# Outer products of a convolution kernel's tables on 64x32 array tiles, fewer of them issued alone, and wider vector operations

## The chip, the cores and the metric

The kernel runs on one core of one Trainium2 chip. The metric is the device time of one execution in microseconds. Before the change the median of three runs is 1099.31 us (1099.19 to 1099.48).

## The reference, cut to what matters

```python
def _A_ref(u, log_A_real, A_imag, C_real, C_imag, log_dt, D_skip):     # u: [1, 2048, 576], tables: [576, 128]
    dt = jnp.exp(log_dt)
    A = -jnp.exp(log_A_real) + 1j * A_imag
    C = (C_real + 1j * C_imag) * dt[:, None]
    P = jnp.exp((A * dt[:, None])[:, :, None] * pos[None, None, :])
    K = 2.0 * jnp.einsum("dn,dnl->dl", C, P).real                      # one filter of 2048 taps per channel
    y = irfft(rfft(u_t, 2 * L) * rfft(K, 2 * L))[:, :, :L]             # causal convolution, channel by channel
    return y + u * D_skip

def reference(...):
    xn = layernorm(A_u)
    s = _A_ref(xn, ...)
    g = silu(gelu(layernorm(xn) @ w1 + b1) @ w2 + b2)                  # 576 -> 4608 -> 576
    return x + s * g
```

Two bodies of work meet only in the last line: a gated two-layer network (by far the most multiplications), and a long convolution whose filter K is itself computed, for every channel, from 128 complex modes.

## The kernel before, in words

**The network.** The tokens are taken in four blocks of 512 (`TB`), two at a time, the hidden units in 12 groups of 3 x 128 (`NG`, `G`). One of the 48 slots is one group for one block: `layer1` (L617) makes three 128x512 results in PSUM, `hidden` (L653, L656, L659) turns each into gelu and splits it into a high and a low float32r part, and `layer2` (L680) multiplies these by the second weights; VectorE adds the result to `acc` (L690). Every product is made of three float32r products, high x high, high x low and low x high.

**The convolution** goes through a transform of 32 x 64 points in chunks of `CH` = 96 channels, six in all (`chunk`). Per chunk: `x1` (L1099) and `k1` (L1130) are the first stage, on the input and on the filter; `s2` (L1160) is the second, on array tiles of 64 rows and 32 columns, followed by the complex products in frequency (`copy`, `prod`, `sums`, L1169 to L1182); `inverse` (L1202) goes back, on tiles of 32 rows and 64 columns; `i1` (L1228) is the last stage. Between stages data is turned by 32x32 transposes (L1107, L1138, L1213).

**The filter's tables.** Channels are taken in 36 blocks of 16 (`SB`). `load_par` (L896, GpSimd's DMA queue) fetches the block's parameters, the 128 modes on the 128 partitions. `tables` then makes phases (L914 to L926), sines (L931, L933), magnitudes (L939) and, in `weigh` (L950 to L956), two weighted tables: `U` (32 columns per channel) and `v` (64 columns per channel), each with a real and an imaginary part. `kgen` (L995) makes each channel's filter as an outer product over the modes, U by v: 2048 taps as 32 x 64. It is 32 float32 matmuls per block, each contracting over all 128 partitions into 32 columns of the array, so four channels stand side by side. ScalarE copies the result out (L1000). `w` has two buffers; `U` and `v` have one each, so the weighing of block b waits for the product of block b-1.

**The order of the work** is fixed when the program is built. `Order` keeps a model time of each engine with durations written by hand, and pins every engine's instructions into the order in which it places them. The layer matmuls form the backbone. After them `pe_turns` looks at the steps of the other lines that TensorE must do. A step of `x1`, `k1`, `s2` or `i1` may carry a guest: `ride` takes the next ready product of `kgen`, and `lead` issues it into the spare columns (384 to 511) of the host's own PSUM tile. A product that finds no host is issued alone after `ALONE` = 12 us of model time past the moment it was ready, or after 3 us if the next block's sines have been placed and the block is due (`DUE`). `KG` = 1.03 us is what the model adds to a host for a guest.

Line numbers are those of the profile. The functions that the diff touches:

Of the kernel before, what the change touches and what calls it, by code (L numbers as in the profile page):

```python
# [18 lines left out]
P = 128  # L19
# [3 lines left out]
CH = 96  # L23
# [187 lines left out]
def mixer_kernel(ctx, tc, u, log_a_real, a_imag, c_real, c_imag, log_dt, d_skip, w1, b1, w2, b2,  # L211
# [38 lines left out]
    idp = sb.tile([P, P], F32, name="idp")  # L250
# [112 lines left out]

    def table_memory():

        t = [sb.tile([P, 2, SB, NV], F32, name="w", bufs=2) for _ in range(2)]
        t = [x.rearrange("p k c t -> p (k c t)") for x in t + [sb.tile([P, 2, SB, 64], F32, name="v")]]
        return [t[k // 3][:, k % 3 * D:(k % 3 + 1) * D] for k in range(8)]
# [418 lines left out]
    def params():  # L787
# [8 lines left out]
        dt = sb.tile([P, 2, SB, 32], F32, name="U").rearrange("p a b c -> p (a b c)")[:, :D]  # L796
# [94 lines left out]
    def load_par(b):  # L891
        if b == NB:
            return
        PAR[b] = sb.tile([P, SB, NPAR], F32, name="par", bufs=2)

        nc.gpsimd.dma_start(PAR[b].rearrange("p (g i) k -> p g (i k)", g=4), dram(  # L896
            par_s, (b // 3 * 48 + b % 3 * 4) * NPAR, [[D * NPAR, P], [12 * NPAR, 4], [1, 4 * NPAR]]))
# [7 lines left out]
    def tables(b):  # L905

        T = {}

        def phase(k):
            if k == 0:
                T["w"] = sb.tile([P, 2, SB, NV], F32, name="w", bufs=2)
                nc.vector.tensor_mul(T["w"][:, 1], bc(PAR[b][:, :, 0], 2, NV), bc(tv, 1, SB))  # L914
            else:
                u = T["w"][:, 1, :, 33:]
                nc.vector.tensor_add(u, u, bc(PAR[b][:, :, 1], 2, 32))

        def whole():
            nc.scalar.activation(T["w"][:, 0].bitcast(I32), T["w"][:, 1], AF.Copy)  # L920

        def frac():
            nc.vector.tensor_sub(T["w"][:, 1], T["w"][:, 1], T["w"][:, 0].bitcast(I32))

        def fold():
            nc.scalar.activation(T["w"][:, 0], T["w"][:, 1], AF.Abs)  # L926

        def sin(k):
            w = T["w"][:, k]
            if k == 0:  # L930
                nc.scalar.activation(w, w, AF.Sin, bias=halfpi[:, 0:1], scale=-TWO_PI)  # L931
            else:
                nc.scalar.activation(w, w, AF.Sin, scale=TWO_PI)  # L933

        def mags(k):
            if k == 0:
                T["m"] = sb.tile([P, SB, NM], F32, name="mg")
            n, e1, e8 = ((8, E1, E8), (4, E64, E512))[k]
            nc.vector.tensor_mul(T["m"][:, :, 64 * k:64 * k + 8 * n].rearrange("p c (i j) -> p c i j", i=n),  # L939
                                 bc(PAR[b][:, :, e8:e8 + n], 3, 8), bc(PAR[b][:, :, e1:e1 + 8], 2, n))  # L940

        def weigh(k, part):

            if k == 0 and part == 0:
                T["v"] = sb.tile([P, 2, SB, 64], F32, name="v")
                T["U"] = sb.tile([P, 2, SB, 32], F32, name="U")
                TAB[b] = (T["U"], T["v"])
            w, v, m = T["w"], T["v"], T["m"]
            if part == 0:
                nc.vector.tensor_mul(T["U"][:, k], w[:, k, :, 33:], m[:, :, 64:])  # L950
            elif part == 1:
                nc.vector.tensor_mul(v[:, k, :, :32], w[:, k, :, 32:0:-1], m[:, :, :32])
            elif k == 0:
                nc.vector.tensor_mul(v[:, k, :, 32:], w[:, k, :, :32], m[:, :, 32:64])
            else:
                nc.vector.scalar_tensor_tensor(v[:, k, :, 32:], w[:, k, :, :32], -1.0, m[:, :, 32:64],  # L956
                                               op0=OP.mult, op1=OP.mult)

        n = SB * 32
        f = lambda g, *a: lambda: g(*a)  # L960
        return ([step(None, 10.0 if b < 6 else 4.5, lambda: load_par(b), mark=("par", b), need=[("pack", b * SB // PK)]
                      + ([("mags", b - 2)] if b > 1 else [("xn", k) for k in range(8, NT)])),
                 step("DVE", dve(SB * NV), f(phase, 0), need=[("wu", b - 2, 1)] if b > 1 else []),
                 step("DVE", dve(n), f(phase, 1)), step("ACT", act(SB * NV), whole),
                 step("DVE", dve(SB * NV), frac), step("ACT", act(SB * NV), fold, mark=("fold", b))],
                [step("ACT", act(SB * NV), f(sin, 0), need=[("fold", b)], mark=("sin", b, 0), tbl="sin"),
                 step("ACT", act(SB * NV), f(sin, 1), mark=("sin", b, 1), tbl="sin")],
                [step("DVE", dve(2 * n), f(mags, 0), need=[("par", b)]),
                 step("DVE", dve(n), f(mags, 1), mark=("mags", b))]
                + [step("DVE", dve(n), f(weigh, k, part), need=[("sin", b, k)] + ([("kg", b - 1)] if b else []),  # L970
                        mark=("wu", b, k) if part == 2 else None) for k in range(2) for part in range(3)])

# [9 lines left out]
    def kgen(b):  # L982
# [3 lines left out]
        def mm(tile=None):  # L986
# [5 lines left out]
            for i in range(SB // 4):  # L992
                for ri in range(2):
                    for g in range(4):
                        nc.tensor.matmul(q[32 * g:32 * g + 32, i // 2, i % 2 * 64:i % 2 * 64 + 64], U[:, ri, 4 * g + i, :],  # L995
                                         v[:, ri, 4 * g + i, :], start=ri == 0, stop=ri == 1, skip_group_check=True)
# [6 lines left out]
        return [step("PE", KG + 0.2, mm, need=need + [("wu", b, 1)], cv=1, mark=("kg", b)),  # L1003
# [23 lines left out]
    def chunk(c):  # L1027
# [41 lines left out]
        def in_parts(which, i, get, m, need):  # L1069

            def high():
                a = sb.tile([P, 2, 4 * CH], F32R, name="pr").rearrange("p t c -> p (t c)")
                b = sb.tile([P, 2, 4 * CH], F32R, name="ys", bufs=2).rearrange("p t c -> p (t c)")
                PARTS2[which, i] = [t.rearrange("p (c b) -> p c b", b=m) for t in (a, b)]
                nc.scalar.activation(PARTS2[which, i][0], get(), AF.Copy)

            def low():
                a, b = PARTS2[which, i]
                nc.vector.tensor_sub(b, get(), a.bitcast(F32))

            n = 768 if which == "k" else 2000
            four.append(step("ACT", act(n), high, need=need))
            four.append(step("DVE", dve(n), low, mark=(which + "p", c, i)))

        def x1(i):
# [3 lines left out]
            def mm():  # L1089
# [4 lines left out]
                lead(q)  # L1094
                for n, (f, x) in enumerate(((0, a), (0, b), (1, a))):
                    for e in range(2):
                        for v in range(2):
                            r = slice(64 * v, 64 * v + 64)
                            nc.tensor.matmul(Q[24 * v][:, e], FP[0][r, f, 0], x[r, 12 * e:12 * e + 12],  # L1099
                                             start=n == 0, stop=n == 2, skip_group_check=True)  # L1100
            add("PE", X1, mm, cv=2, mark=("x1", c, i), need=[("xp", c, i)])
            if i + 1 < CH // 48:
                four.append(step(None, 5.0, lambda: load(i + 1), mark=("xl", c, i + 1)))
            for d0 in (0, 24):
                for e in range(2):
                    c0 = 48 * i + d0 + 12 * e
                    add("DVE", 0.65, lambda d0=d0, e=e, c0=c0: nc.vector.transpose(  # L1107
                        A2[:, :, 0, c0:c0 + 12].rearrange("p k d r -> p d k r"), Q[d0][:, e]), cv=-e)

        def k1(i):  # L1110
# [7 lines left out]
            in_parts("k", i, lambda: KT[c, i], 64, [("k1", c, i - 1) if i else ("x1", c, CH // 48 - 1)])  # L1118
# [18 lines left out]
            for g in range(4):  # L1137
                add("DVE", 0.65, lambda g=g: nc.vector.transpose(  # L1138
                    A2[:, :, 1, 48 * i + 12 * g:48 * i + 12 * g + 12].rearrange("p k d r -> p d k r"),
                    Q[g // 2 * 2][:, g % 2]),  # L1140
                    cv=-(g % 2))

        def s2(p):
# [5 lines left out]
            def mm():  # L1149
# [5 lines left out]
                for i in range(2):  # L1155
                    for ri in range(2):
                        for q in range(4):
                            for f in range(2):
                                r = slice(64 * f, 64 * f + 64)
                                nc.tensor.matmul(Q[i][32 * q:32 * q + 32, f, 2 * ri:2 * ri + 2],  # L1160
# [6 lines left out]
            def copy(i):  # L1167
                KK[i] = sb.tile([P, 2, 2, CH], F32, name="kk")
                nc.scalar.activation(KK[i], Q[i][:, :, 1::2], AF.Copy)  # L1169

            def prod(i):

                PR[i] = sb.tile([P, 2, 4 * CH], F32, name="pr").rearrange("p t (a b d) -> p t a b d", a=2, b=2)
                for t in range(2):
                    nc.vector.tensor_mul(PR[i][:, t], bc(Q[i][:, t, 0::2], 2, 2), bc(KK[i][:, t], 1, 2))

            def sums(i):
# [3 lines left out]
                nc.vector.tensor_sub(y[:, i, 0], x[:, :, 0, 0], x[:, :, 1, 1])  # L1181
                nc.vector.tensor_add(y[:, i, 1], x[:, :, 0, 1], x[:, :, 1, 0])  # L1182
            for i in range(2):
                two.append(step("ACT", act(4 * CH), lambda i=i: copy(i), need=[("s2", c, p)]))
                two.append(step("DVE", 0.95, lambda i=i: prod(i), cv=-1))
                two.append(step("DVE", 0.63, lambda i=i: sums(i), mark=("sum", c, p) if i else None))
# [548 lines left out]
```

## Time and profile before

| | |
|---|---|
| median of the runs | 1099.31 us |
| the profiled execution | 1101.59 us, its span 1099.8 us |
| TensorE matmuls | busy 99% of the span, granted clock 0.999 |
| TensorE weight loads | 87% |
| VectorE, ScalarE, GpSimd | 84%, 63%, 17% |
| DMA | 138 MB, 126 GB/s on average |
| products of `kgen` | 2304 records of 219 ns |

A matmul's busy time includes its passage through the array, so consecutive matmuls overlap: what one costs is read from start to start. Tiles of the array work side by side, and their records overlap too. A float32 matmul of the source appears as two records, a float32r matmul as one; each record of a matmul has a weight load of its own beside it, listed as PEld.

### The profile page before, as it was taken

The page shows a single profiled execution, that of the slowest core. Times are in us where ns is not written, and L with a number is a line of the kernel's source. Part 1 is how long each engine was busy: PE and PEld are TensorE (multiplying, and loading weights), DVE is VectorE, ACT ScalarE, POOL GpSimd, SP SyncE. Part 2 cuts the span into 40 slices and gives each one's busy share as a digit, 9 for nine tenths or more (in the row PEclk, how much of TensorE's full clock was granted, in tenths as well). Part 3 has the DMA queues.
Part 4 walks back from the last instruction along what each step waited for, and adds up shares of the span by engine and source line. Part 5 has one row for each costly group of instructions (what it writes and reads, how often), then busy time and mean ns, then how long its engine had stood idle before and what let it go on. Part 6 is the DMA issues. An engine that isn't in the chain of part 4 may idle for free.

```text
span 1099.8 us, 27208 instructions
## 1 busy us (share of the span) xinstructions
PE 1089.1 (99%) x11445; PEld 953.2 (87%) x11445; DVE 918.8 (84%) x1514; ACT 698.0 (63%) x1044; POOL 184.0 (17%) x255
## 2 busy tenths in 40 slices
PE   8999999999999999999999999999999999999997
PEld 7889989889888888888898888888888888888897
DVE  7698678979998899999999998898998986766356
ACT  6485699867667675676865857566775754324233
POOL 4557211161110100001100000000100012110220
PEclk9999999999999999999999999999999999999999
DMA  8836656735434252355623315242333426453453
GB/s 222 242 131 169 219 173 197 215 71 130 152 115 152 53 112 57 100 128 149 154 51 95 96 56 126 39 143 59 94 89 78 145 66 178 117 178 107 128 148 94
DMA packets 139651, 138.23 MB, mean 126 GB/s; under 512 B 88952, under 2 KB 105016, under 8 KB 138952
## 3 DMA queue, kind: packets, MB, share of 16 engines
q1 hardware_dynamic: 124664, 85.49, 29.6%
q0 software_dynamic: 14384, 50.27, 14.8%
q8 instruction: 89, 1.46, 0.6%
q10 hardware_dynamic: 480, 0.74, 0.3%
q14 instruction: 34, 0.28, 0.1%
HBM read 102.17 MB, written 36.63 MB: 126 GB/s over the span
## 4 chain that ended last, share of the span: by engine, by line
PE 95%; DMA 2%; SPq 2%; DVE 1%; issue 0%; ACTq 0%; ACT 0%; DVEq 0%
PE mxb L680 21%; PE mxa L680 21%; PE mxa L617 20%; PE mxb L617 20%; PE cv L995 3%; PE cv L1160 3%; PE cv L1202 2%; PE cv L1228 2%; PE cv L1130 1%; PE cv L1099 1%; SPq L808 1%; DMA w<-in_A_u_dram 1%; DMA acc<-in_A_u_dram 0%; DVE st L407 0%; DMA h<-in_B_b_dram 0%
## 5 line engine op out<-in xcount | busy, mean ns | idle before, releaser
L659 DVE TENSOR_TENSOR hl<-h,hh 128x512 fp32r<-128x512 f32 x144 | 98.8, 689 | 89.0 <-ACT hh L656 88.3
L680 PE MATMUL mxb<-w2h,hl 128*128 128x288 f32 x576 | 170.2, 295 | 1.8 <-DVE hl L659 1.8
L680 PE MATMUL mxb<-w2h,hh 128*128 128x288 f32 x576 | 171.6, 298 | 0.0
L680 PE MATMUL mxa<-w2h,hh 128*128 128x288 f32 x573 | 170.8, 298 | 0.0
L680 PE MATMUL mxb<-w2l,hh 128*128 128x288 f32 x576 | 169.5, 294 | 0.0
L680 PE MATMUL mxa<-w2h,hl 128*128 128x288 f32 x573 | 169.2, 295 | 0.0
L680 PE MATMUL mxa<-w2l,hh 128*128 128x288 f32 x573 | 168.6, 294 | 0.0
L653 ACT ACTIVATE h<-mxa,b1t 128x512 f32<-128x512 f32 x73 | 50.2, 689 | 110.9 <-PE mxa L617 109.9
L680 PEld LDWEIGHTS mxa<-w2h,hh 128*128 128x128 f32 x573 | 107.6, 188 | 6.6 <-issue 3.5
L680 PEld LDWEIGHTS mxb<-w2h,hh 128*128 128x128 f32 x576 | 108.1, 188 | 5.7 <-issue 1.8
L680 PEld LDWEIGHTS mxb<-w2h,hl 128*128 128x128 f32 x576 | 108.1, 188 | 2.3 <-DVE hl L659 2.3
L680 PEld LDWEIGHTS mxb<-w2l,hh 128*128 128x128 f32 x576 | 108.1, 188 | 0.6
L680 PEld LDWEIGHTS mxa<-w2l,hh 128*128 128x128 f32 x573 | 107.6, 188 | 0.7
L680 PEld LDWEIGHTS mxa<-w2h,hl 128*128 128x128 f32 x573 | 107.5, 188 | 0.1
L896 POOL DMA_DIRECT2D par<-par_s x36 | 27.8, 773 | 462.9 <-DVE mg L939 458.4
L656 ACT ACTIVATE hh<-h 128x512 fp32r<-128x512 f32 x144 | 90.6, 630 | 3.6
L653 ACT ACTIVATE h<-mxb,b1t 128x512 f32<-128x512 f32 x71 | 48.9, 689 | 68.8 <-PE mxb L617 66.4
L690 DVE TENSOR_TENSOR acc<-mxa,acc 128x576 f32<-128x576 f32 x87 | 65.5, 752 | 31.2 <-PE mxa L680 30.9
L617 PE MATMUL mxa<-XH,w1h 128*128 128x512 f32 x284 | 79.1, 400 | 0.0
L690 DVE TENSOR_TENSOR acc<-mxb,acc 128x576 f32<-128x576 f32 x88 | 66.1, 752 | 15.2 <-PE mxb L680 14.8
L617 PE MATMUL mxb<-XH,w1h 128*128 128x512 f32 x280 | 77.7, 399 | 0.0
L617 PE MATMUL mxa<-XL,w1h 128*128 128x512 f32 x284 | 76.1, 390 | 0.0
(269 smaller groups left out, 2483.8 us busy)
## 6 DMA issues: line engine op xcount, KB each, us to landing
raw<-in_B_w_dram SPq DMA_DIRECT2D x72, 288.0 KB, 3.4
raw<-in_B_w_dram SPq DMA_DIRECT2D x96, 192.0 KB, 3.8
par_s<-A POOLq DMA_DIRECT2D x4, 2160.0 KB, 8.2
par<-par_s POOLq DMA_DIRECT2D x36, 240.0 KB, 3.4
f2t<-f2q SPq DMA_DIRECT2D x24, 256.0 KB, 3.4
g2t<-g2p SPq DMA_DIRECT2D x24, 256.0 KB, 4.1
bias<-XR SPq DMA_DIRECT2D x42, 128.0 KB, 3.7
raw<-in_B_w_dram SPq DMA_DIRECT2D x48, 96.0 KB, 3.9
```

Source lines behind the costliest of these rows:

```text
L617: nc.tensor.matmul(q, a, b, start=j == 0 and i not in BEGUN, stop=j == len(ops) - 1, skip_group_check=True)
L653: nc.scalar.activation(t, q, AF.Gelu_apprx_tanh, bias=b1t[:, k:k + 1], scale=1.0)
L656: LAST[0] = nc.scalar.activation(hh[:, i], t, AF.Copy)
L659: nc.vector.tensor_sub(hl[:, i], t, hh[:, i].bitcast(F32))
L680: nc.tensor.matmul(q[:, dh, :288], a[:, i, c], b[:, i, d], start=i == 0 and k == 0 and not alone, stop=i == G - 1 and k == 2)
L690: nc.vector.tensor_add(o, q[:, dh:dh + n, :288], b)
L808: nc.sync.dma_start(r[32 * g:32 * g + 32].rearrange("c (b n) -> c b n", n=32), dram(src[k], 32 * g, [[N, 32], [32 * N, D // 32], [1, 32]]))
L896: nc.gpsimd.dma_start(PAR[b].rearrange("p (g i) k -> p g (i k)", g=4), dram(par_s, (b // 3 * 48 + b % 3 * 4) * NPAR, [[D * NPAR, P], [12 * ...
L995: nc.tensor.matmul(q[32 * g:32 * g + 32, i // 2, i % 2 * 64:i % 2 * 64 + 64], U[:, ri, 4 * g + i, :], v[:, ri, 4 * g + i, :], start=ri == ...
L1160: nc.tensor.matmul(Q[i][32 * q:32 * q + 32, f, 2 * ri:2 * ri + 2], m[r, 4 * i + q, 32 * ri:32 * ri + 32], A2[r, 4 * p + 2 * i + q // 2, :, ...
L1202: nc.tensor.matmul(QI[q // 2][64 * f:64 * f + 64, q % 2, i], MAT["g2t", p + i // 2][r, i % 2, f, ri], YS[p + i // 2][0][r, i % 2, ri, f], ...
L1228: nc.tensor.matmul(Q[h][64 * y:64 * y + 64, t], g1t.rearrange("p a e -> p (a e)"), A2[:, k:k + 2, 1].rearrange("p i d r -> p i r d"), star ...
```

## The change

- `kgen`: each outer product is split over the modes into two halves of 64, so that it runs on tiles of 64 rows by 32 columns; partitions 0 to 63 work for one half of the block's channels, 64 to 127 for the other. Four matmuls (real and imaginary, two halves) now add into one result where there were two. `load_par` places the parameters accordingly, with four DMAs per block, each with half as long runs.
- `U` and `v` disappear as tiles of their own. `w` is 32 columns wider, holds both, and still has two buffers; `weigh` works in place, in four operations rather than six. The phases of block b now wait for the product of block b-2, and the weighing no longer waits for a product.
- `ALONE` goes from 12 to 20 us, and the shorter wait now needs the next block's tables to be finished.
- `x1` issues its guest behind its own matmuls rather than ahead of them. Its input is first turned by one more ScalarE copy into `xt`; the split into parts then reads it straight.
- Pairs of VectorE operations are joined: transposes after `x1` and `k1`, the two halves of `prod`, the difference and the sum in `sums` (with a negated copy on ScalarE). `s2` writes its output in another order for this.
- Memory is laid out anew: `idp` shares the buffer of `f2t`, `dt` that of `ys`, and the rows held in table memory at the start lie four to a tile.

```diff
-    idp = sb.tile([P, P], F32, name="idp")
+    idp = sb.tile([P, 4, P], F32, name="f2t")[:, 0]
...
+    def table_tile():
+        return sb.tile([P, 2, SB, 32 + NV], F32, name="w", bufs=2)
...
-        dt = sb.tile([P, 2, SB, 32], F32, name="U").rearrange("p a b c -> p (a b c)")[:, :D]
+        dt = ys_tile().rearrange("p i a b c -> p (i a b c)")[:, :D]
...
-        nc.gpsimd.dma_start(PAR[b].rearrange("p (g i) k -> p g (i k)", g=4), dram(
-            par_s, (b // 3 * 48 + b % 3 * 4) * NPAR, [[D * NPAR, P], [12 * NPAR, 4], [1, 4 * NPAR]]))
+        for h in range(2):
+            for e in range(2):
+                nc.gpsimd.dma_start(
+                    PAR[b][64 * h:64 * h + 64, 8 * e:8 * e + 8].rearrange("p (g i) k -> p g (i k)", g=4), dram(
+                        par_s, (64 * e * D + b // 3 * 48 + b % 3 * 4 + 2 * h) * NPAR,
+                        [[D * NPAR, 64], [12 * NPAR, 4], [1, 2 * NPAR]]))
...
+                T["v"] = table_tile()
+                T["w"] = T["v"][:, :, :, 32:]
...
+            if part == 0:
+                TAB[b] = (T["w"][:, :, :, 33:], T["v"][:, :, :, :64])
             w, v, m = T["w"], T["v"], T["m"]
             if part == 0:
-                nc.vector.tensor_mul(T["U"][:, k], w[:, k, :, 33:], m[:, :, 64:])
+                nc.vector.tensor_mul(v[:, :, :, :32], w[:, :, :, 32:0:-1], bc(m[:, :, :32], 1, 2))
             elif part == 1:
-                nc.vector.tensor_mul(v[:, k, :, :32], w[:, k, :, 32:0:-1], m[:, :, :32])
-            elif k == 0:
-                nc.vector.tensor_mul(v[:, k, :, 32:], w[:, k, :, :32], m[:, :, 32:64])
+                nc.vector.tensor_mul(w[:, :, :, 33:], w[:, :, :, 33:], bc(m[:, :, 64:], 1, 2))
+            elif part == 2:
+                nc.vector.tensor_mul(w[:, 0, :, :32], w[:, 0, :, :32], m[:, :, 32:64])
...
-            for i in range(SB // 4):
-                for ri in range(2):
+            for i in range(2):
+                for k in range(4):
+                    ri, e = divmod(k, 2)
                     for g in range(4):
-                        nc.tensor.matmul(q[32 * g:32 * g + 32, i // 2, i % 2 * 64:i % 2 * 64 + 64], U[:, ri, 4 * g + i, :],
-                                         v[:, ri, 4 * g + i, :], start=ri == 0, stop=ri == 1, skip_group_check=True)
+                        for h in range(2):
+                            f, t = slice(64 * h, 64 * h + 64), 8 * e + 2 * g + i
+                            nc.tensor.matmul(q[32 * g:32 * g + 32, h, 64 * i:64 * i + 64], U[f, ri, t, :], v[f, ri, t, :],
+                                             start=k == 0, stop=k == 3, skip_group_check=True)
...
+            def turn():
+                T["x"] = sb.tile([P, 24, m], F32, name="xt")
+                nc.scalar.activation(T["x"], get(), AF.Copy)
...
-                lead(q)
                 for n, (f, x) in enumerate(((0, a), (0, b), (1, a))):
...
+                lead(q)
             add("PE", X1, mm, cv=2, mark=("x1", c, i), need=[("xp", c, i)])
...
-                nc.scalar.activation(KK[i], Q[i][:, :, 1::2], AF.Copy)
+                KK[i] = sb.tile([P, 2, 3, CH], F32, name="kk")
+                nc.scalar.activation(KK[i][:, :, :2], Q[i][:, :, :1:-1], AF.Copy)
+                nc.scalar.activation(KK[i][:, :, 2], Q[i][:, :, 3], AF.Copy, scale=-1.0)
...
-                for t in range(2):
-                    nc.vector.tensor_mul(PR[i][:, t], bc(Q[i][:, t, 0::2], 2, 2), bc(KK[i][:, t], 1, 2))
+                nc.vector.tensor_mul(PR[i], bc(x, 2, 2), k)
...
-                nc.vector.tensor_sub(y[:, i, 0], x[:, :, 0, 0], x[:, :, 1, 1])
-                nc.vector.tensor_add(y[:, i, 1], x[:, :, 0, 1], x[:, :, 1, 0])
+                nc.vector.tensor_add(y[:, i].rearrange("p a t d -> p t a d"), x[:, :, :, :CH], x[:, :, :, CH:])
...
-    ALONE, DUE = 12.0, (160.0, 950.0)
+    ALONE, DUE = 20.0, (160.0, 950.0)
...
-                    wait = ("sin", b + 1, 1) not in od.marks or od.t["PE"] < DUE[0] + b * (DUE[1] - DUE[0]) / NB
+                    wait = ("wu", b + 1) not in od.marks or od.t["PE"] < DUE[0] + b * (DUE[1] - DUE[0]) / NB
```

More of the change, by code (lines that the diff above doesn't have):

```diff
@@ L969, in tables @@
                  step("DVE", dve(n), f(mags, 1), mark=("mags", b))]
-                + [step("DVE", dve(n), f(weigh, k, part), need=[("sin", b, k)] + ([("kg", b - 1)] if b else []),
-                        mark=("wu", b, k) if part == 2 else None) for k in range(2) for part in range(3)])
+                + [step("DVE", dve((2, 2, 1, 1)[part] * n), f(weigh, part), need=[("sin", b, 1)],
+                        mark=("wu", b) if part == 3 else None) for part in range(4)])
     KT = {}
@@ L1069, in in_parts, with source @@
         def in_parts(which, i, get, m, need):
+            T = {}
+            def turn():
+                T["x"] = sb.tile([P, 24, m], F32, name="xt")
+                nc.scalar.activation(T["x"], get(), AF.Copy)
+            def source():
+                return get() if which == "k" else T["x"].rearrange("p c b -> p (c b)")
             def high():
[L1072 to L1075, printed above, removed]
+                T["a"] = sb.tile([P, 2, 4 * CH], F32R, name="pr").rearrange("p t c -> p (t c)")
+                T["b"] = sb.tile([P, 2, 4 * CH], F32R, name="ys", bufs=2).rearrange("p t c -> p (t c)")
+                PARTS2[which, i] = [T[k].rearrange("p (c b) -> p c b", b=m) for k in "ab"]
+                nc.scalar.activation(T["a"], source(), AF.Copy)
             def low():
[L1078 to L1083, printed above, removed]
+                nc.vector.tensor_sub(T["b"], source(), T["a"].bitcast(F32))
+            if which == "x":
+                four.append(step("ACT", act(2000), turn, need=need))
+            four.append(step("ACT", act(768), high, need=need if which == "k" else ()))
+            four.append(step("DVE", dve(768), low, mark=(which + "p", c, i)))
         def x1(i):
@@ L1104, in x1 @@
             for d0 in (0, 24):
[L1105 to L1108, printed above, removed]
+                c0 = 48 * i + d0
+                add("DVE", 0.9, lambda d0=d0, c0=c0: nc.vector.transpose(
+                    A2[:, :, 0, c0:c0 + 24].rearrange("p k d r -> p d k r"), Q[d0]), cv=-1)
         def k1(i):
@@ L1136, in k1 @@
             add("PE", X1, mm, cv=2, mark=("k1", c, i), need=[("kp", c, i)] + ([("i1", c - 1)] if c and i == 0 else []))
[L1137 to L1141, printed above, removed]
+            for g in (0, 2):
+                add("DVE", 0.9, lambda g=g: nc.vector.transpose(
+                    A2[:, :, 1, 48 * i + 12 * g:48 * i + 12 * g + 24].rearrange("p k d r -> p d k r"), Q[g]), cv=-1)
         def s2(p):
@@ L1180, in sums @@
                 x, y = PR[i], Y[0]
[L1181 to L1182 removed]
+                nc.vector.tensor_add(y[:, i].rearrange("p a t d -> p t a d"), x[:, :, :, :CH], x[:, :, :, CH:])
             for i in range(2):
[L1184 to L1186 removed]
+                two.append(step("ACT", act(4 * CH) + act(2 * CH), lambda i=i: copy(i), need=[("s2", c, p)]))
+                two.append(step("DVE", dve(8 * CH), lambda i=i: prod(i), cv=-1))
+                two.append(step("DVE", dve(4 * CH), lambda i=i: sums(i), mark=("sum", c, p) if i else None))
             if p % 2:
```

27 lines of the change are left out of this document (11 added, 16 removed).

## The prediction

> **What bounds the kernel now.** I read the page from the top: the busy times, the slices, then the chain that ended last. After that I read the waits of TensorE, the groups of its matmuls, and the timeline around single products.
>
> ```profile
> span 1099.8 us, 27208 instructions
> ...
> PE 1089.1 (99%) x11445; PEld 953.2 (87%) x11445; DVE 918.8 (84%) x1514; ACT 698.0 (63%) x1044; POOL 184.0 (17%) x255
> ...
> PE 95%; DMA 2%; SPq 2%; DVE 1%; issue 0%; ACTq 0%; ACT 0%; DVEq 0%
> ```
>
> TensorE is busy 99% of the span, and 95% of the chain is TensorE. VectorE, at 84%, looks close behind. The list of TensorE's waits (us in total, times, longest) says whether it matters:
>
> ```profile
> PE mxb L680 <- DVE hl L659: 1.8, 2, 1.2
> ```
>
> The longest row of that list: TensorE waits 1.8 us in all for VectorE's hidden parts. So the time is the sum of what TensorE is given to do. VectorE and ScalarE count only if they become late, and an edit that merely shortens their work has at most those few microseconds to win. The change is therefore priced in TensorE time.
>
> **The products as they are.** The groups of matmuls give the shapes: tile rows*columns, then partitions x streamed columns. A float32 matmul of the source stands as two records, so the 32 matmuls of one product are 64 records, each a weight load with its matmul: a pair.
>
> ```profile
> L995 PE MATMUL cv<-v,U 128*32 128x64 f32 x2304 | 39.6, 221 | 0.0
> L1160 PE MATMUL cv<-A,f2t 64*32 64x192 f32 x1536 | 38.6, 332 | 0.0
> ...
> L1202 PE MATMUL cv<-ys,g2t 32*64 32x96 f32 x1536 | 21.9, 253 | 0.0
> ```
>
> A product alone between layer matmuls:
>
> ```profile
> 153.98 0.39 PE L617 MATMUL mxa<-XR,w1r 128*128 128x512 f32 x1
> 154.21 0.39 PE L617 MATMUL mxa<-XR,w1s 128*128 128x512 f32 x1
> 154.53 1.10 PE L995 MATMUL cv<-v,U 128*32 128x64 f32 x64
> 155.56 1.20 PE L617 MATMUL mxb<-XH,w1h 128*128 128x512 f32 x4
> 156.59 0.39 PE L617 MATMUL mxb<-XL,w1h 128*128 128x512 f32 x1
> ```
>
> The columns are the start, the length and the count. From the start of one layer matmul (154.21) to that of the fifth after it (156.59) is 2.38 us. Five steps of 0.23 (153.98 to 154.21) are 1.15, so the lone product costs 1.23 us. From its first matmul's start to its last one's are 1.10 less the 0.22 of one, 0.88 us: 63 steps of 14.0 ns. Four column tiles take turns, so one tile is used again every 56 ns.
>
> The same product riding ahead of the second stage, and that stage without a guest:
>
> ```profile
> 309.85 0.39 PE L617 MATMUL mxb<-XR,w1s 128*128 128x512 f32 x1
> 310.17 1.10 PE L995 MATMUL cv<-v,U 128*32 128x64 f32 x64
> 311.20 1.62 PE L1160 MATMUL cv<-A,f2t 64*32 64x192 f32 x64
> 312.75 0.40 PE L680 MATMUL mxa<-w2h,hh 128*128 128x288 f32 x1
> 312.99 0.29 PE L680 MATMUL mxa<-w2l,hh 128*128 128x288 f32 x1
> ...
> 973.52 0.39 PE L617 MATMUL mxb<-XR,w1s 128*128 128x512 f32 x1
> 973.84 1.59 PE L1160 MATMUL cv<-A,f2t 64*32 64x192 f32 x64
> 975.36 0.40 PE L680 MATMUL mxa<-w2h,hh 128*128 128x288 f32 x1
> 975.59 0.30 PE L680 MATMUL mxa<-w2l,hh 128*128 128x288 f32 x1
> ```
>
> With the guest 309.85 to 312.99 is 3.14 us; without it 973.52 to 975.59 is 2.07. The guest costs 1.07 us, 0.16 less than alone. Of this, 0.15 is a pause between the two tile shapes: the product's last matmul starts at 310.17 + 0.88 = 311.05, the stage's first at 311.20.
>
> **The change, part by part.** (1) *Tile shape.* Each contraction over 128 rows becomes two over 64 rows, on eight tiles instead of four. The multiplications stay the same, but a product is now 64 source matmuls, 128 pairs, of the same 64 streamed columns. If only the tiles bound, eight tiles reused every 56 ns would take a pair every 7.0 ns, and 128 pairs 0.90 us, no change from 0.88. The question is whether TensorE can be fed pairs that fast for so long. No row shows this shape with 64 columns. The nearest row is the inverse (L1202), the only burst of 128 pairs on eight tiles. Its row of the timeline; then a window at its start, whose columns are the length, and busy time with the count for matmuls and for weight loads:
>
> ```profile
> 325.66 1.83 PE L1202 MATMUL cv<-ys,g2t 32*64 32x96 f32 x128
> ```
>
> ```profile
> 325.65:325.95 0.30, 0.29 (x24) 0.29 (x32) 1.00 0.00 0
> ```
>
> From the first matmul's start to the last one's are 1.83 less 0.25 for one (the group's mean), 1.58 us: 127 steps of 12.4 ns. In the first 0.29 us 32 loads and 24 matmuls have started, the loads 9 ns apart. The other 104 matmuls take 1.58 - 0.29 = 1.29 us, again 12.4 ns each, although they have only to follow loads that began well ahead. I read this as a stock of about 32 pairs that is ready when the burst begins, and a supply of one pair per 12.4 ns behind it. The product of today needs a pair every 14.0 ns and the second stage one every 20 (1.59 less 0.33, over 63), both slower than this supply; that is why neither shows it.
>
> The Trainium skill, "TensorE: Matmul & The Clock Gate", Terms and Part 1, gives TensorE a queue of 64 instructions, which is 32 pairs; the knee in the trace agrees. The skill's "TensorEngine Tiling (Array Packing)", Instruction Overhead, speaks against this edit: a matmul carries about 60 cycles however few its columns, and one should not split a dimension that is already small. By that figure at 2.4 GHz (25 ns, an estimate) 128 serial pairs would take 3.2 us and the kernel about 80 us more; the 14.0 ns of the trace contradict it as a serial price, since tiles overlap, so it gets no chance of its own.
>
> So the new product has the bounds 0.90 us (tiles alone) and 1.58 (the inverse's whole pace). I take the inverse's supply with the faster tiles: 32 pairs at 7.0 ns are 0.22, 96 at 12.4 are 1.19, together 1.41 us. That is 0.53 more than 0.88. It is nearer to the upper end because the count of pairs, not their width, is what that row shares with the new product.
>
> (2) *Who carries the products.* In the instruction order of the two built programs, before: 18 products alone and 18 riding (12 on the second stage, 5 on k1, 1 with x1). After: 7 alone, 14 on the second stage, 5 on k1, 6 behind x1, 4 ahead of i1. Eleven fewer alone save 11 x 0.16 = 1.8 us. For the 14 on the second stage the shape no longer changes between guest and host; the pause of 0.15 shrinks to one step of about 0.02, so 14 x 0.13 = 1.8 us saved.
>
> (3) *VectorE and ScalarE.* The groups that change, VectorE's, then ScalarE's (busy us, mean ns of one):
>
> ```profile
> L950 DVE TENSOR_TENSOR U<-w,mg 128x512 f32<-128x512 f32 x72 | 49.2, 683 | 3.7 <-PE cv L995 2.3 <-ACT w L931 0.7
> ...
> L939 DVE TENSOR_TENSOR mg<-par 128x1024 f32<-128x1024 f32 x36 | 44.0, 1222 | 0.7
> ...
> L1079 DVE TENSOR_TENSOR ys<-xc,pr 128x768 fp32r<-128x768 f32 x12 | 24.7, 2056 | 1.8 <-ACT pr L1075 1.6
> ...
> L1138 DVE STREAM_TRANSPOSE A<-cv 128x384 f32<-128x384 f32 x48 | 24.5, 556 | 2.7 <-PE cv L1130 2.7
> ...
> L1079 DVE TENSOR_TENSOR ys<-kt,pr 128x768 fp32r<-128x768 f32 x12 | 11.1, 927 | 0.0
> ```
>
> ```profile
> L1075 ACT ACTIVATE pr<-xc 128x768 fp32r<-128x768 f32 x12 | 25.2, 2101 | 12.4 <-DMA xc<-xn_s 12.3
> L1169 ACT ACTIVATE kk<-cv 128x384 f32<-128x384 f32 x48 | 23.1, 482 | 24.4 <-PE cv L1160 13.5 <-DVE pr L1175 10.9
> ```
>
> VectorE: the subtraction that read the turned data reads it straight, 12 x (2.06 - 0.93) = 13.5 us less. Per block six weighings of 0.68 become two of 1.22 and two of 0.68, 36 x 0.28 = 10 less. Pairs of 384-element operations become one of 768: at the 0.93 of a 768-element row against 2 x 0.55, some 0.18 each for 48 transposes and 48 multiplications, 17 less; the joined sums about 7. Together some 48 us of 919. ScalarE: the added turn costs 12 x 2.1 and the copies behind it save 12 x 1.26; the added negated copy is about 0.3 (0.48 for 384 elements, half of it) x 48 = 14. It gains about 25 us on 698, 66% of the span. TensorE waited 1.8 us for VectorE, so I price all of this at nothing, with at most 2 us to win. Its cover is the idle time of ScalarE; if that went, gelu (L653) would come late.
>
> (4) *Loads of parameters.* One issue per block becomes four:
>
> ```profile
> L896 POOL DMA_DIRECT2D par<-par_s x36: 747/757/1000, 123.0 to 868.8; - x36
> ```
>
> That is 108 more issues at 0.757, 82 us on an engine that is busy 17%. The last part lands 2.3 us later. Behind it stand VectorE's phases of that block; these now also wait for the product of two blocks earlier, which is later still, so nothing is charged. Other issues on GpSimd's queue (stores of s, reordered matrices) wait 2.3 us longer at most, with no tight reader. The renamed buffers at the start (idp, dt, the rows held in table memory) change no matmul of the first slots.
>
> **Sum.** 22 products at +0.53 are 11.7; 14 at 0.53 - 0.13 are 5.6; 11 fewer alone give -1.8: +15.5 us. The profiled execution took 1101.6 (span 1099.8) against a median of 1099.3, so overheads outside the span are about 1.8; added to the median, 1099.3 + 15.5 = **1114.8**.
>
> **Rivals.** *Tiles alone bound* (faster). If pairs arrive every 7.0 ns throughout, a product takes 0.90: 36 x 0.02 = +0.7, -1.8 and -1.8 make -2.9, **1096.4**. It decides where 36 times the growth falls below 3.6, at a product of 0.98 us or 7.7 ns a pair. For it: the first pairs of the inverse come at about 10 ns or less. Against it: its later ones never do on average. *The inverse's full pace*: a product of 1.58, 36 x 0.70 - 3.6 = +21.6, **1120.9**. For it: same count, same tiles in number. Against it: its wider loads and columns.
>
> *Instructions run short.* Instructions arrive by their own queue:
>
> ```profile
> q8 instruction: 89, 1.46, 0.6%
> ```
>
> That is 16.4 KB a packet; 1.46 MB over 22890 instructions are 64 B, so 256 a packet, and one product is now a packet by itself. If each riding product (29) paid 0.5 us waiting for a packet on top of the forecast, +14.5, **1129**. Against it: the inverse uses a packet in 1.6 us and shows no gap. *The change does not do what it says*: rides cost the same and VectorE's relief is hidden; that is the forecast without the two savings, 36 x 0.53 = +19.1, **1118.4**.
>
> **How the numbers follow.** Forecast with a product of 1.2 to 1.55: 0.55 (own range 1107 to 1120, 36 x 0.32 or 0.67 less 3.6). Tiles alone: 0.25. Full pace or no saving: 0.13. Instructions short or a late engine: 0.07. The range 1095 to 1123 reaches just past the second case and leaves out its lower side and the last case. A measurement of this kernel tells 0.2% (2.2 us) from no change; the tiles-alone case at -2.9 is just over it, so I split its 0.25 into 0.19 faster and 0.06 same, add 0.02 to each for intermediate products, and leave 0.71 slower.
>
> **What would show it.** In the changed profile: the product's merged row of 128 pairs from first start to last, 1.41 us (0.90 and 1.58 for the rivals), with a knee after about 32 pairs; no pause before the second stage's first matmul; VectorE some 48 us less busy and ScalarE 25 more; TensorE at 99% as before. A product near 0.9 us would make the prediction wrong at step (1); TensorE waiting several microseconds for hl, par or a packet would make it wrong at (3), (4) or the last rival.

## The result, and the profile after

The changed kernel takes 1132.52 us (median of five runs, 1130.49 to 1134.10) against 1099.48 for the kernel before, measured beside it: a ratio of 1.030, 95% interval 1.028 to 1.031. It is slower by 33 us where 15.5 were forecast. The direction was right; the time lies outside the range given.

The page of the changed kernel, first its busy times and chain, then one group of matmuls and the instruction queue:

```profile
span 1131.5 us, 31806 instructions
...
PE 1107.0 (98%) x13749; PEld 971.2 (86%) x13749; DVE 895.1 (79%) x1298; ACT 726.2 (64%) x1109; POOL 245.5 (22%) x363
...
q8 instruction: 107, 1.75, 0.7%
...
PE 92%; DVE 3%; issue 2%; SPq 2%; DMA 1%; ACT 0%; ACTq 0%; DVEq 0%
```

VectorE has become lighter (919 to 895 us) and ScalarE heavier (698 to 726). TensorE falls from 99% to 98% of a longer span, and a new entry, "issue", holds 2% of the chain: time in which the engine waited for nothing that the profile shows. The waits of TensorE say where it is. First the weight loads of the second stage before the change, then of the same stage after it (us in total, times, longest):

```profile
PEld cv L1160 <- issue: 2.6, 11, 0.4
```

```profile
PEld cv L1174 <- issue: 19.9, 19, 2.5
...
PE cv L1174 <- issue: 13.5, 9, 2.2
```

Before, eleven short pauses of 0.4 us at most, the switches of tile shape. After, pauses of up to 2.5 us. One of the rides in the timeline of the changed kernel:

```profile
468.17 0.29 PE L682 MATMUL mxa<-w2h,hl 128*128 128x288 f32 x1
468.40 1.48 PE L1003 MATMUL cv<-w 64*32 64x64 f32 x128
469.68 1.23 PE L1174 MATMUL cv<-A,f2t 64*32 64x192 f32 x42
472.13 0.88 PE L1174 MATMUL cv<-A,f2t 64*32 64x192 f32 x22 [1.22 <-issue]
472.94 0.40 PE L682 MATMUL mxb<-w2h,hh 128*128 128x288 f32 x1
```

The product's 128 pairs take 1.27 us from first start to last (1.48 less 0.22, the group's mean matmul). The second stage follows at once, but stops in its midst after 42 of 64 records, with nothing to wait for in the program.

To see where the whole difference lies I added up, for every pair of neighbouring matmul records, the time from start to start, and put it to the stage that both belong to (or to "switches" where they differ):

| us | before | after | |
|---|---|---|---|
| products | 31.7 | 46.1 | +14.4 |
| second stage | 30.7 | 50.1 | +19.4 |
| k1 | 12.1 | 13.2 | +1.1 |
| switches between stages | 48.1 | 43.4 | -4.7 |
| layers, their small gaps included | 865.5 | 867.1 | +1.6 |
| x1, inverse, i1, the start | 104.1 | 104.0 | -0.1 |

"The start" is the first 60 us. The sum is +31.7, the difference of the spans (1131.5 - 1099.8). Two thirds of it is the second stage and k1, whose matmuls the change did not touch in number or size. I also counted TensorE's instructions from 0 at the start of the trace: loads, matmuls and the few semaphore instructions of its queue. After the first 60 us the changed kernel has twelve gaps of over 0.6 us, from the start of one load or matmul to the start of the next. One is a wait for VectorE's addition to `acc`. The other eleven all end at an instruction whose number is 256k + 193 (k is a whole number). The instruction queue brings 16.4 KB, 256 instructions, a packet; the last packet started 2.2 to 2.8 us before the end of each of these gaps, and took 0.9 to 1.4 us of them itself. Other DMA traffic is not what held it up: in the last 3 us before the end of six of the eleven gaps the other queues started no more than 4 KB. For the ride above, the DMA activity from 465.5 to 472.5 us in 40 slices of 0.175 us:

```profile
GB/s 199 129 59 23 12 0 0 0 0 0 0 0 0 0 0 0 0 0 0 0 0 0 0 94 0 0 0 0 0 0 0 0 0 0 0 0 0 0 0 0
...
q8 instruction: 1, 0.02, 1.0%
```

The slice with 94 GB/s (94 x 0.175 = 16.4 KB) is the packet, at about 469.6. TensorE goes on at 472.13, 2.5 us later.

### The profile page after: what moved, and what is told of

Read it like the earlier page. It is cut to its first block, busy times and chain, and to the rows that moved or that the text cites. A ratio compares the mean times of both kernels' runs of the same rounds, so it can differ in the third digit from the quotient of the medians.

```text
span 1131.5 us, 31806 instructions
## 1 busy us (share of the span) xinstructions
PE 1107.0 (98%) x13749; PEld 971.2 (86%) x13749; DVE 895.1 (79%) x1298; ACT 726.2 (64%) x1109; POOL 245.5 (22%) x363
## 4 chain that ended last, share of the span: by engine, by line
PE 92%; DVE 3%; issue 2%; SPq 2%; DMA 1%; ACT 0%; ACTq 0%; DVEq 0%
PE mxb L682 20%; PE mxa L682 19%; PE mxa L619 19%; PE mxb L619 19%; PE cv L1003 5%; PE cv L1174 4%; PE cv L1217 2%; PE cv L1243 2%; PE cv L1146 1%; PE cv L1115 1%; SPq L810 1%; DMA w<-in_A_u_dram 1%; DMA acc<-in_A_u_dram 0%; SPq L385 0%; PE mxb L602 0%
## 5 line engine op out<-in xcount | busy, mean ns | idle before, releaser
L900 POOL DMA_DIRECT2D par<-par_s x144 | 88.7, 632 | 367.1 <-DVE mg L946 301.4
```

The lines of the kernel that those rows point to most:

```text
L900: nc.gpsimd.dma_start(PAR[b][64 * h:64 * h + 64, 8 * e:8 * e + 8].rearrange("p (g i) k -> p g (i k)", g=4), dram(par_s, (64 * e * D + b // ...
```

## The experiments

**Theory A**: a product is now 256 instructions with its weight loads, a whole packet; where it is followed at once by the second stage's 128, TensorE uses up what it holds faster than packets come, and stands still at a packet's boundary. **Theory B**: the second stage waits for something else that the change moved (tables, parameters, ScalarE's copies, the order of queues). **Rival C**: the 64x32 tiles themselves stall when two bursts of them follow each other.

The table holds the sums of the kind above, for the profiled execution of each run; "layers" includes small gaps. The time is the median. The profiled executions of e2, e4 and e10 were some 4 us slower than their medians, that of e3 2 us faster. The first 60 us are left out, so e3's late start, 12 us, stands in its layers.

| us | time | products | second stage | switches | layers |
|---|---|---|---|---|---|
| before | 1099.5 | 31.7 | 30.7 | 48.1 | 865.5 |
| changed | 1132.5 | 46.1 | 50.1 | 43.4 | 867.1 |
| e1 old tiles | 1101.6 | 31.8 | 30.7 | 45.2 | 868.2 |
| e2 new tiles alone | 1123.6 | 45.5 | 40.9 | 48.6 | 866.9 |
| e3 shift | 1132.1 | 45.9 | 32.1 | 43.5 | 882.9 |
| e4 no riders | 1131.2 | 52.0 | 30.9 | 53.6 | 872.1 |
| e5 old tiles twice | 1137.4 | 63.9 | 35.3 | 48.7 | 862.4 |
| e6 cheap shift | 1121.1 | 45.6 | 31.8 | 43.8 | 874.4 |
| e7 old tiles, old rule | 1100.2 | 31.8 | 30.8 | 46.9 | 865.1 |
| e8 half the modes | 1095.6 | 23.1 | 31.2 | 43.3 | 871.5 |
| e9 before, shifted | 1099.8 | 31.7 | 30.6 | 48.2 | 863.6 |
| e10 no riders, planned | 1132.0 | 45.7 | 30.7 | 52.3 | 881.3 |

**e1, the tile shape undone.**

```diff
-            for i in range(2):
-                for k in range(4):
-                    ri, e = divmod(k, 2)
+            for i in range(SB // 4):
+                for ri in range(2):
                     for g in range(4):
...
+                        nc.tensor.matmul(q[32 * g:32 * g + 32, i // 2, i % 2 * 64:i % 2 * 64 + 64], U[:, ri, 4 * g + i, :],
+                                         v[:, ri, 4 * g + i, :], start=ri == 0, stop=ri == 1, skip_group_check=True)
```

> The changed kernel with one part undone: products on 128x32 tiles again (64 pairs each, 128 instructions) and parameters loaded by one DMA; riders, doubled tables, wide VectorE operations stay. Theory A, TensorE's instructions arrive too slowly for 256-instruction products (a stall wherever two boundaries of 256 instructions are crossed within some 3.5 us): no gap over 0.5 us left, a product back at 0.88 us, time 1097 to 1099, that is the 1099.5 of before less up to 1.8 for eleven fewer lone products. Theory B, the second stage waits for something else that the change moved (tables, parameters, ScalarE's extra copies, queue order): the gaps of 1 to 2.5 us inside the second stage stay, 1115 to 1120.

Measured: 1101.58, ratio 1.0017 (1.0008 to 1.0026). The second stage is back at 30.7 us and the wait reads as before:

```profile
PEld cv L1167 <- issue: 2.1, 8, 0.4
```

So the tile shape, with its four loads of parameters, carries the loss, and theory B falls for everything that stayed in this kernel. The time missed its bracket by 2.6 us: the lone products saved 2.9 in switches, but the layers lost 2.7 to small waits. Two of these, 0.5 and 0.6 us from start to start, end at 256k + 193 as well.

**e2, the tile shape alone in the kernel before** (the reverse of e1's diff, with the four parameter DMAs).

> The kernel before with that one part alone: products on 64x32 tiles (128 pairs) with four parameter DMAs; order of work, tables and VectorE as before (18 products alone, 18 riding). Theory A: a product takes 1.27 us from first start to last, 36 x 0.39 = +14; the pause of 12 rides on the second stage falls, -1.6; about half of those 12 rides meet two boundaries and stall by 1 to 2.5 us, +10: 1099.5 + 22 = 1121 to 1125. Theory B: +14 - 1.6 without gaps, 1112.

Measured: 1123.59, as theory A has it. The products give +13.8 and the second stage +10.2; all eight gaps over 0.6 us, seven in the second stage and one just behind a k1 that carried a product, end at 256k + 193. The 1.6 us less that I expected for the pauses do not show in the switches (48.6 against 48.1), where that last gap of 1.6 us is counted.

**e3 and e6, the same instructions at another place in their packets.** e3 put 64 full-width matmuls of 8 columns ahead of the warm-up, e6 the same 128 instructions on 32-column tiles:

```diff
+    zf = zero.bitcast(F32)
+    for k in range(32):
+        g = 32 * (k % 4)
+        nc.tensor.matmul(qb[g:g + 32, 0, :8], zf[:, g:g + 32], zf[:, :8], start=True, stop=True)
     warm_up(16)
```

> The changed kernel with 64 tiny matmuls (8 columns of zeros, 128 instructions with their loads) added ahead of the warm-up; nothing else moves. They run while TensorE waits for the first data, so by themselves they cost 0 to 3 us. Theory A: every boundary of 256 instructions falls 128 instructions earlier in the work; the ten riding second stages that stalled mostly do not any more and the others do, the sum of gaps falls from 21 us to some 7, and the time from 1132.5 to 1116 to 1122. Theory B: the same second stages stall as in the changed kernel, 1132 to 1136.

> The changed kernel with 128 instructions ahead of the warm-up again, but on 32-column tiles of 8 columns, which take about 1 us together where the full-width ones of the earlier shift took 14. Theory A: the gaps move as in that run (second stage 32 us instead of 50), nothing else changes: 1132.5 - 18 + 1 = 1114 to 1118. If instead the earlier run's equal time came from the work itself and not from its slow start, 1130 to 1134.

e3 gave 1132.14, no change, which by the letter speaks for theory B. The trace shows two changes that cancel: the second stage fell from 50.1 to 32.1 us, but the added group kept TensorE for 13.8 us (216 ns a matmul), and the first layer matmul started at 24.86 us, not 12.95. The group in the costliest groups of e3:

```profile
L1307 PE MATMUL mxa<-XL 128*128 128x8 f32 x64 | 13.8, 354 | 1.3 <-POOL XL L1298 1.3
```

My price of 0 to 3 us for them was wrong. e6 put that right (first layer matmul at 13.36) and gave 1121.14, 11.4 less than the changed kernel, with the same program behind it. The ride shown above, in e6's timeline, and then the waits:

```profile
467.94 1.48 PE L1003 MATMUL cv<-w 64*32 64x64 f32 x128
469.30 1.60 PE L1174 MATMUL cv<-A,f2t 64*32 64x192 f32 x64
470.83 0.40 PE L682 MATMUL mxb<-w2h,hh 128*128 128x288 f32 x1
```

```profile
PEld mxa L682 <- issue: 8.0, 13, 3.5
...
PEld cv L1174 <- issue: 3.1, 10, 0.6
```

The ride runs through: 2.89 us from the product to the next layer matmul, 4.54 in the changed kernel. The 18 us of the second stage are gone; some 7 came back in the layers, among them one gap of 3.5 us just behind a ride. Three gaps over 0.6 us are left that no other engine explains, and all three end at 256k + 193 again. That is why e6 stayed above its bracket. No wait of the program depends on where an instruction stands in its packet, so theory B falls, and rival C with it: both bursts and all 14 rides are the same as in the changed kernel.

**e9, the control**: the same 128 instructions ahead of the kernel before.

> Control: the kernel before with the same 128 cheap instructions ahead of its warm-up. Theory A: before, two boundaries of 256 instructions hardly ever fall within 3.5 us, so moving them does next to nothing; the tiny matmuls cost 0 to 1 us: 1099.5 to 1101.5. If the shift by itself made a kernel faster (another start, another clock), 1090 or less.

Measured: 1099.84, ratio 0.9998 (0.9987 to 1.0008). In the kernel before, a shift by itself does nothing.

**e5, the dose on the old tiles**: the kernel before, each product issued twice over itself.

```diff
-            for i in range(SB // 4):
+            for _ in range(2):
+                for i in range(SB // 4):
...
```

> The kernel before, but every product is issued twice over itself on its 128x32 tiles (128 pairs, 256 instructions, 14 ns a pair; the result is the same). By itself that is 36 x 0.90 = +32. Theory A (slow arrival of instructions, whatever the tile): some of the 12 riding second stages now hold two boundaries of 256 instructions within 3 us, gaps of 0.5 to 1.5 us in them, +5 to +10: 1136 to 1142, and every gap ends at the same place of a 256-instruction block. Rival C (the 64x32 tiles themselves stall when two bursts of them follow each other): no gaps, 1132.

Measured: 1137.42. The products cost +32.2 by their count, the second stage +4.6. One ride:

```profile
465.04 0.91 PE L1162 MATMUL cv<-A,f2t 64*32 64x192 f32 x32
466.88 0.91 PE L1162 MATMUL cv<-A,f2t 64*32 64x192 f32 x32 [0.93 <-issue]
```

All five gaps over 0.6 us end at 256k + 193. The same stop, on 128x32 tiles with one load of parameters per block, in a kernel that the change never touched: it is the number of instructions, not the shape. Rival C is gone.

**e8, half of each product left out** (the sum runs over 64 of the 128 modes), on the new tiles.

```diff
-                for k in range(4):
+                for k in (0, 2):
...
-                                             start=k == 0, stop=k == 3, skip_group_check=True)
+                                             start=k == 0, stop=k == 2, skip_group_check=True)
```

> The changed kernel with half of each product left out: the second half of the modes of each partition group is not multiplied, so the filter is summed over 64 of the 128 modes. 64 pairs, 128 instructions per product on the same 64x32 tiles. Theory A: a product takes 0.6 us, kernel and gaps follow the number of instructions, no gap over 0.6 us in a riding second stage: 1099.5 - 36 x 0.28 - 3.6 + 2 to 4 of small waits = 1088 to 1091. Rival C (the tiles): gaps in the riding second stages of a good part of the 21 us, 1098 to 1108.

Measured: 1095.60. The products fell by 8.6 us and no riding second stage has a gap over 0.6; that is theory A. The total missed by 5 us, because the layers rose by 6. Waits for VectorE and ScalarE are part of that (1.7 us for gelu, 1.6 for VectorE), and one gap of 0.9 us in a layer ends at 256k + 193.

**e4 and e10, no riders.** e4 issued every product alone as soon as it was ready; e10 waited 3 us (the second pair of lines; e4 has 0 there) and had the model count 1.62 us for it (`KG` = 1.42 and 0.2).

```diff
-        if not kl["steps"] or kl["steps"][0]["eng"] != "PE" or host["mark"][0] == "inv":
+        if True or not kl["steps"] or kl["steps"][0]["eng"] != "PE" or host["mark"][0] == "inv":
...
-    ALONE, DUE = 20.0, (160.0, 950.0)
+    ALONE, DUE = 3.0, (160.0, 950.0)
```

> The changed kernel, but no product rides: all 36 are issued alone as soon as they are ready. A lone product of 1.27 us costs 1.62 with the switches of tile shape; 36 x 1.62 = 58 against 18 x 1.23 + 18 x 1.07 = 41 before: +17. Theory A: 256 instructions of a product between layer matmuls seldom hold two boundaries, gaps under 3 us in all: 1116 to 1120. Theory B: gaps in the second stage as in the changed kernel, 1135 or more.

> The changed kernel with every product alone again, but placed with more care than in the earlier run: the model counts 1.62 us for it and it waits 3 us after it is ready, so that TensorE should not stand waiting for VectorE. Theory A: gaps from instructions under 3 us, +17 for 36 lone products of 1.62 us, 2 to 5 of small waits: 1118 to 1122. If VectorE's waits are as in the earlier run (12 us), 1128 to 1132. Theory B (the second stage waits for something the change moved): gaps inside the second stage of 10 us or more.

Measured: 1131.23 and 1131.95, where theory A gave 1116 to 1122; e10's time lies where its expectation put it if VectorE's waits stayed. Theory A's mechanism held for the second stage, which is at 30.9 and 30.7 us, as before the change. Its total did not: in e10 the layers rose by 16 us, and in e4 TensorE stood 5.8 us for a table and 5.8 us for VectorE's other work. e4's waits:

```profile
PE cv L1003 <- DVE w L961: 5.8, 1, 5.8
PE mxa L682 <- DVE acc L692: 3.6, 2, 2.3
PE mxb L682 <- DVE hl L661: 2.2, 1, 2.2
```

Issuing all 36 products alone moved the other engines' work against the layers. In e10 one stop was left as well, by the list of its waits:

```profile
PE mxa L682 <- issue: 2.7, 1, 2.7
```

It came three layer matmuls behind a lone product, with no second burst beside it, and it too ends at 256k + 193. So these two runs say that no rider means no stop in the second stage; they also say that a lone product can be stopped at a boundary.

**e7, the old rule for lone products with the old tiles.**

```diff
-    ALONE, DUE = 20.0, (160.0, 950.0)
+    ALONE, DUE = 12.0, (160.0, 950.0)
...
-                    wait = ("wu", b + 1) not in od.marks or od.t["PE"] < DUE[0] + b * (DUE[1] - DUE[0]) / NB
+                    wait = ("sin", b + 1, 1) not in od.marks or od.t["PE"] < DUE[0] + b * (DUE[1] - DUE[0]) / NB
```

> The changed kernel with old tiles and loads and also the old rule for lone products (12 us, next block's sines): what is left of the change is doubled tables, wide VectorE operations, the turned copy and the guest behind x1. If the 4 us of small waits that the run with old tiles showed come from the longer wait for riders, 1098 to 1100; if they come from the rest, 1101 to 1103.

Measured: 1100.24, ratio 1.0004 (0.9995 to 1.0013). This is 0.2 us above the first bracket. Doubled tables, wide VectorE operations, the turned copy and the guest behind x1 together are worth nothing that can be measured. The small waits of e1 point to the longer wait for riders: the layers take 865.1 us here and 868.2 there. Of the kernels here that compute the whole result, none beat the kernel before.

## Why the prediction came out too small

**What bounds the kernel** held in part. No other engine made TensorE wait much longer than before (1.0 us for `acc` is the longest wait for one after the start). But "the time is the sum of what TensorE is given to do" did not hold: in the eleven gaps, 18.4 us from start to start, TensorE had work and stood still.

**Step (1), the price of a product**, was right in kind and too high. I had 1.41 us from the inverse's pace; it is 1.27, +0.39 a product and +14.4 in all, not 19.1. A slight knee is there. A lone product in the changed kernel, and a window on its first 0.30 us (length, then busy time and count of matmuls, weight loads, VectorE, ScalarE, GpSimd):

```profile
152.63 1.49 PE L1003 MATMUL cv<-w 64*32 64x64 f32 x128
```

```profile
152.62:152.92 0.30, 0.30 (x34) 0.30 (x34) 0.30 (x2) 0.30 (x1) 0.00 (x0) 1.00 0.00 0
```

One of the 34 matmuls is a layer matmul still running. The first 33 of the product start within 0.27 us, 8.3 ns apart; the other 95 take 1.27 - 0.27 = 1.00, 10.5 ns each. The term that was too large is the 12.4 ns taken from the inverse; whether its wider tiles are the reason no run separates. The Trainium skill's queue of 64 instructions ("TensorE: Matmul & The Clock Gate", Part 1) fits this knee too; no run here shows what sets the 10.5 ns behind it.

**Step (2), the riders' savings**, was right: 3.6 us forecast, 4.7 found in the switches. The pause ahead of the second stage is the predicted single step (in the ride above the stage starts 0.01 us after the product's last matmul).

**Steps (3) and (4)** cost nothing, as said. ScalarE's 28 us and GpSimd's 62 us more were hidden; the layers grew by 1.6 us. VectorE lost 24 us instead of the 48 that I worked out. The multiplication of the second stage before the change, and the joined one in the changed kernel:

```profile
L1175 DVE TENSOR_TENSOR pr<-cv,kk 128x384 f32<-128x384 f32 x96 | 48.7, 549 | 2.0 <-ACT kk L1169 1.8
```

```profile
L1191 DVE TENSOR_TENSOR pr<-cv,kk 128x768 f32<-128x768 f32 x48 | 45.7, 953 | 22.2 <-ACT kk L1184 22.1
```

Joining the pairs saved 3.0 us in all (48.7 - 45.7) where I had some 8.6, and the wait ahead of them grew by 20. I had priced a single operation at 0.55 us, but neighbours overlap: 96 x 0.549 are 52.7 us, and the engine was busy for 48.7.

**The step that failed is the sum's term for the supply of instructions: it was put at nothing.** The rival "instructions run short" had it, at 14.5 us for all 29 riders at 0.5 us each, with 7 in 100 shared with a late engine, and I dismissed it by the inverse. The second stage and k1 grew by 20.5 us by these stops and the slow clock behind the longest of them (below), and they struck few riders hard rather than all a little: of the eleven stops nine lie in the second stage, one in k1 and one in the layer just behind a ride. My argument against it, that the inverse uses a packet in 1.6 us without a gap, was true of the inverse and did not carry over. The inverse is followed by layer matmuls at 0.13 to 0.23 us an instruction pair, a riding product by another 128 instructions at once; I take this for the difference, though e10's lone product, with only layer matmuls behind it, was stopped too. With step (1) as measured and the stops added, the sum is 14.4 + 20.5 - 4.7 + 1.6 = 31.8. That the forecast missed by no more is partly luck: the product's price was 4.7 us too high, and e6 shows that mere placement moves the time by 11 us.

One stop cost more than its length. Around the longest one (892.60 to 903.00 us; columns are length, busy times with counts, granted clock, DMA):

```profile
892.60:896.50 3.90, 1.81 (x133) 1.42 (x133) 3.80 (x5) 0.38 (x1) 0.42 (x1) 1.00 1.06 271
896.57:899.00 2.43, 2.43 (x61) 1.81 (x60) 0.91 (x1) 0.00 (x0) 0.00 (x0) 0.59 0.39 107
899.00:900.40 1.40, 1.40 (x8) 1.40 (x7) 0.29 (x1) 0.99 (x3) 0.00 (x0) 0.50 0.10 38
900.40:903.00 2.60, 2.60 (x18) 2.47 (x18) 1.34 (x2) 0.68 (x2) 0.00 (x0) 0.99 0.26 80
```

After the 2.5 us of that stop the granted clock is 0.50 for 3.4 us, about 1.7 us more (an estimate: half of 3.4). The Trainium skill, "TensorE: Matmul & The Clock Gate", Part 1, has such a fall to half speed after an idle window of about 3.4 us; the 0.50 and the 3.4 us agree, though here a stop of 2.5 us was enough. The other ten gaps of the changed kernel did not trip it, and in e3 a stop of 2.5 us did not either.

**Which boundaries stop TensorE.** In all eleven stops of the changed kernel the packet started 0.6 to 1.5 us after TensorE had passed the boundary before, and from that boundary to the end of the stop were 3.1 to 3.9 us. Eleven other pages of 256 were used up within 3 us without a stop, a lone product's 1.3 us among them; for each of these the packet had started 0.7 to 3.6 us before TensorE reached the page. I read this so: the following page is asked for about when what runs ahead of TensorE enters a page, early in slow stretches and late behind a burst, and is there some 3.5 us later. It does not cover everything: at the longest stops of e3, e6 and e10 the packet started only 2.6, 3.9 and 2.8 us after the boundary, and 5.2, 6.4 and 4.8 us passed from there to the end of the stop. The Trainium skill, "Runtime: NRT & Kernel Launch", Instruction fetch mechanics, says that an engine fetches the next block of 256 instructions while it executes the present one, and that a crossing is mostly hidden. The 256 agrees; the hiding holds at the eleven pages used up without a stop and fails at the eleven stops.

**Open.** The request itself was not seen, so the reading above is argued from packets and not shown. It is also not shown what fills the 2.2 to 2.8 us from a packet's start until its first instruction runs, beyond the packet's own 0.9 to 1.4.

## What to carry to other kernels

Count instructions, not only multiplications: splitting each contraction in two for twice as many array tiles doubled the loads and matmuls here, and a burst of hundreds of tiny ones outran the packets that bring them. Price a rider together with its host: two bursts that are harmless apart can meet a boundary between them. A stop that the profile calls "issue" is checked by moving all instructions by half a packet: if the stop moves, the supply is what to look at.

## What the runs showed of the hardware that I had not expected

TensorE can stop where a new 256 of its instructions begin (16.4 KB, one packet of its instruction queue) when bursts use them up quickly: gaps of 0.9 to 2.5 us in the changed kernel, moved but not removed by 128 instructions at the start, and worth up to 11 us of 1132 by mere placement (e6). Full-width matmuls of only 8 columns took 216 ns each at the very start of e3 (13.8 us for 64), against 1.0 us for as many instructions on 32-column tiles in e6.
